# Batch index 1 of an attention and feed-forward kernel: where three groups of vector work stand

## The chip, the core and the metric

The kernel runs on one core of one Trainium2 chip. The time is that of one execution of the whole program on the device, in microseconds. Four engines work beside each other and wait for each other through semaphores: PE multiplies matrices, DVE (VectorE) and ACT (ScalarE) do elementwise work, and SP issues the transfers between memory and the core. POOL (GpSimd) does almost nothing here.

## The reference

For each of 8 batch indices and 8 heads, 576 positions are softly assigned to 32 memory slots by `phi`; keys and values are averaged into these slots, the queries attend to them, and the joined heads (512 wide) go through a feed-forward layer with a SiLU. All of it is in float32.

```python
a = phi - np.max(phi, axis=2, keepdims=True)          # over the 576 positions
a = np.exp(a)
a = a / (np.sum(a, axis=2, keepdims=True) + 1e-09)
k_m = np.einsum('bhsm,bhsd->bhmd', a, k)
v_m = np.einsum('bhsm,bhsd->bhmd', a, v)
scores = np.matmul(q, k_m.transpose(0, 1, 3, 2)) / np.sqrt(64)
attn = softmax(scores)                                 # over the 32 slots
x = np.matmul(attn, v_m)                               # heads joined: 4608 x 512
h = x @ w_in                                           # 512 x 2048
out = (h * (1.0 / (1.0 + np.exp(-h)))) @ w_out         # 2048 x 512
```

## The kernel before, in words

**Batch index after batch index.** While the feed-forward work of index b runs on PE, the attention work of index b + 1 is done beside it in small steps, its *events*. For index 1, which this text is about, the feed-forward work is cut into 16 *slots* (`fc`), one for each 128 of the 2048 hidden columns.

**One slot of index 1.** PE forms the *first product* h (12 L701 matmuls over 2 x 288 positions). ACT applies the SiLU: L728 for 512 positions into a buffer g, L730 for the other 64 into `gleft`. For accuracy each f32 operand is held as a *high* part, rounded to the matmul's type, and a *remainder*. DVE writes g's high part (L718, a cast) and g's remainder (L720). Then the slot's events run, and then PE forms the *second product* of the slot before (12 L746 matmuls with the high and low parts of `w_out`). So the order on PE is: first product of slot s, steps of attention, second product of slot s - 1, first product of slot s + 1. There is a single tile for h, so that the next first product waits until L728 and L730 have read it.

**P.** The value part of attention is multiplied into `w_in` beforehand. Its result P is made in four parts, the events `p_mm` (L649 on PE, then L677, P's high part, on ACT, and L679, P's remainder, on DVE). Parts 1, 2 and 3 of index 1 are made in slots 1, 5 and 9, and read from slots 4, 8 and 12 on.

**The keys of index 2.** Its `phi` is loaded near the end of index 0's slots (SP, line 88), when DVE's transposes (L464) have freed the tile's home. Event `phi_max` in slot 1 takes a running maximum (L258, L259, L261 twice), `phi_fold` in slot 2 folds it over the partitions (L286 to L304) and `phi_sub` in slot 2.5 subtracts it (L312 and L315, twice each). The Exp (L319) is an ACT instruction between slots 3 and 4; each change between Exp and SiLU needs a table load on ACT. Event `e_tr` in slot 9 turns the averaged keys and values by PE into the free columns of h and copies them out: L368 for the keys, L369 for the values.

**The forms.** Events `w_forms` make eight *forms* of `w_out`, sums of its quarters that the later indices use. Form j starts in slot 1.5 j + 2 (the third in slot 5.5): on DVE a sum L814 and four more, L818 to L821; then on ACT their high parts (L835) and on DVE their remainders (L836). Form 0 comes in slot 2, form 1 in 3.5, form 5 in 9.5.

**What sets the order.** PE's order, and from index 1 on ACT's, is the order of the program text. DVE's order is made by a scheduler out of data dependences and its own estimate of when inputs are ready; `behind(i, other)` forbids it to put i ahead of other. `last_split[-1]` is the latest remainder of g, `last_p[-1]` the latest remainder of P. In the loop over slots, the names of DVE instructions that an event adds go into `late` if the event is in a list, and `late` instructions are put behind the slot's remainder of g.

Of the kernel before, what the change touches and what calls it, by code (L numbers as in the profile page):

```python
# [19 lines left out]
P = 128  # L20
# [28 lines left out]
def attn_ffn_kernel(  # L49
# [9 lines left out]
    nc = tc.nc  # L59
# [27 lines left out]
    def load(dst, src, few=False, queue=None):  # L87
        i = (queue or nc.sync).dma_start(dst, src)
        if few:
            tc.add_manual_dep(  # L90
                i.ins,
                loads[-DEEP].ins.name,
                mybir.DependencyInfo(mybir.DependencyClass.Sync, mybir.DependencyReason.DATA),
                reason="few at a time",
            )
        loads.append(i)

    @contextmanager
    def in_order(*engines):
        traced = nc.cur_bb.bb.instructions  # L100
        n = len(traced)
        last = {}
        yield last
        for i in list(nc.cur_bb.bb.instructions)[n:]:
            if i.engine in engines:
                if i.engine in last:
                    tc.add_manual_dep(
                        i,
                        last[i.engine].name,
                        mybir.DependencyInfo(mybir.DependencyClass.NoSync, mybir.DependencyReason.DATA),  # L110
                        reason="in_order",
                    )
                last[i.engine] = i
# [6 lines left out]
    raws, cvas, last_silu, last_split, last_kvn, last_turn = {}, {}, [], [], [], []  # L120
# [89 lines left out]
    def banks(b):  # L210
        if b == 0:
            return [ps.tile([P, 512], F32, tag="acc", name=f"first{i}", bufs=NI) for i in range(2)]
        bg = bgtile()
        return [bg[:, 0], bg[:, 1]]

    def beside_h(w):

        return [live["h"][:, i, HALF : HALF + w] for i in range(2)]
# [144 lines left out]
    def e_tr(b):  # L363
        pt = beside_h(P) if b <= 2 else banks(b)
        t = sb.tile([P, 2, NR, M], F32, tag="kvT", name=f"kvT{b}", bufs=2)
        for kind in range(2):
            nc.tensor.transpose(pt[kind][:, :P], kvn[:, kind].rearrange("p g d -> p (g d)"), ident)
        nc.vector.tensor_copy(t[:, 0].rearrange("p r m -> p (r m)"), pt[0][:, :P])  # L368
        nc.scalar.copy(t[:, 1].rearrange("p r m -> p (r m)"), pt[1][:, :P])  # L369
        at[b]["kvT"] = t  # L370

# [251 lines left out]
    pj, wins, last_p = {}, {}, []  # L623
# [173 lines left out]
    def as_f32(x):  # L797
        return x.bitcast(F32)

    def keep(tag, n):  # L800
        t = sb.tile([P, n, DMODEL], F32R, tag=tag, name="kept", bufs=1)
        for i in range(n):
            kept.append(t[:, i])
            kept_at.append((t, i))

    def w_forms(j, step):


        if step == 0:
            while len(kept) < 3 * j + 3:  # L810
                keep(*homes_left.pop(0))
            f = at[0]["forms", j] = sb.tile([P, 2, DMODEL], F32, tag="cva", name="wf", bufs=1)
            c = slice(2 * j, 2 * j + 2)
            i = nc.vector.tensor_tensor(f, as_f32(wo_hi[:, c]), as_f32(wo_lo[:, c]), op=ALU.add)  # L814
            if j < 3:
                behind(i.ins, last_kvn[0] if j == 2 else last_split[-1])
            b11, b12, b21, b22 = (f[:, k, q * Q : (q + 1) * Q] for k in range(2) for q in range(2))
            nc.vector.tensor_tensor(b11, b12, b11, op=ALU.subtract)  # L818
            nc.vector.tensor_tensor(b12, b22, b12, op=ALU.add)
            nc.vector.tensor_tensor(b22, b22, b11, op=ALU.add)  # L820
            nc.vector.tensor_tensor(b21, b22, b21, op=ALU.subtract)  # L821
            return
        f = at[0]["forms", j].rearrange("p k (q f) -> p (k q) f", q=2)
        t1 = sb.tile([P, 1, DMODEL], F32R, tag="cva1", name="t1", bufs=1)
        runs = [[t1, 0, 1]]
        for u in range(3 * j, 3 * j + 3):
            t, i = kept_at[u]
            if t is runs[-1][0]:
                runs[-1][2] = i + 1
            else:  # L830
                runs.append([t, i, i + 1])
        n = 0
        for t, i, e in runs:
            src, to = f[:, n : n + e - i], t[:, i:e]
            nc.scalar.activation(to[:, :, :Q], src, AF.Copy)  # L835
            nc.vector.tensor_tensor(to[:, :, Q:], src, to[:, :, :Q], op=ALU.subtract)  # L836
            n += e - i
        load(saved[j], as_f32(t1[:, 0]))
# [6 lines left out]
    def ffn1s(b, t, j):  # L845
        h = live["h"] = ps.tile([P, 2, 512], F32, tag="h", name="h", bufs=1)
        ahi, alo = (at[b][x][:, :, t * HALF : (t + 1) * HALF] for x in ("ahi", "alo"))
        hi, lo = pj[b, j // 2]
        for i in range(2):
            f = (2 * j + i) * P % JW  # L850
            n = 0
            for wt, a in ((hi, ahi), (hi, alo), (lo, ahi)):
                for p in range(2):
                    nc.tensor.matmul(  # L854
                        h[:, i, :HALF], wt[:, p, f : f + P], a[:, p], start=n == 0, stop=n == 5
                    )
                    n += 1
        return h
# [393 lines left out]
    def behind(i, other):  # L1252
        tc.add_manual_dep(
            i,
            other.ins.name,
            mybir.DependencyInfo(mybir.DependencyClass.NoSync, mybir.DependencyReason.DATA),
            reason="behind",
        )

    def finish(tiles):  # L1260
        if prev is None:
            return
        if prev[0] == "main":
            main_step(prev[1], prev[2], prev[3], tiles)
        elif prev[0] == "left" and tiles[0] == 0:
            if prev[1] < 2:
                left_step(prev[1], prev[2], prev[3])
                t1_load(prev[2])
            else:
                left_st(prev[1], prev[2], prev[3])  # L1270
        elif prev[0] == "st" and tiles[0] == 0:
            st_step(*prev[1:])
# [16 lines left out]
    for b in range(B):  # L1289
        if b == 1:  # L1290
            whole.close()
            ctx.enter_context(in_order(ACT))
        for s in range(NFC if b > 1 else 0):
            t, j = divmod(s, NP)
            h = ffn1s(b, t, j)
            part = forms(b, t, j, h)
            run(b, s)
            finish(range(NI))
            prev = ("st", b, t, j, part)
        for fc in range(NFC if b < 2 else 0):  # L1300
            if b == 0 and fc < 2:
                for part in range(2):
                    for fn, a in events.pop((b, fc + part / 2), []):
                        fn(*a)
                continue
            h = ffn1(b, fc, low_last=b == 1 and fc == 0)
            gs = split(silu(b, fc, h), steps=(2, 1) if fc == NFC - 1 else (0, 1))
            for part in range(2):
                if b == 0:
                    finish((2 * part, 2 * part + 1))  # L1310
                traced = nc.cur_bb.bb.instructions
                n = len(traced)
                late = set()
                for fn, a in events.pop((b, fc + part / 2), []):
                    m = len(nc.cur_bb.bb.instructions)
                    fn(*a)
                    if fn is phi_max or b and fn in (s_max, s_sub, s_sum, s_norm, s_back, s_low):
                        late.update(i.name for i in list(nc.cur_bb.bb.instructions)[m:])
                if b == 0:
                    for i in list(nc.cur_bb.bb.instructions)[n:]:  # L1320
                        if i.engine == ACT:
                            behind(i, last_silu[-1])
                        elif i.engine == DVE and (fc > 10 or i.name in late):
                            behind(i, last_split[-1])
                for i in list(nc.cur_bb.bb.instructions)[n:] if b else ():
                    if i.engine == DVE and i.name in late:
                        behind(i, last_split[-1])
            if b:
                finish(range(NI))
            prev = ("main", b, fc, gs)  # L1330
        if b % 2:
            for n in range(NLS):
                gs = left_split(b, n)
                run(b, NFC + n)
                finish((0, 1, 2, 3))
                prev = ("left", b, n, gs)
# [56 lines left out]
```

## Time and profile before

| | us |
|---|---|
| median of 3 runs | 682.2 (681.66 to 682.36) |
| the profiled execution | 681.68 |
| its span in the trace | 679.9 |
| PE busy | 666.5 (98%) |
| DVE busy | 518.6 (76%) |
| ACT busy | 370.1 (54%) |
| first product of slot 0 of index 1 begins | 105.75 |
| first product of index 2 begins | 201.74 |

A profile row gives the start, the length, the engine, the source line, the operation, `out<-in` by tile names and the shape; `x12` means that twelve instructions are shown as one. What stands in brackets is the idle time of the engine just before, and what ended it. Rows of the waits give the waiting group, whom it waited for, the total, the number and the longest. Instructions of one engine overlap a little, so that the next can start before the length of the last is over.

### The profile page before, as it was taken

The numbers are of one execution on the slowest core, as the hardware profiler recorded it, in microseconds if no ns is written. First come the engines' busy times: TensorE is split into PE (matmuls) and PEld (weight loads), VectorE is DVE, ScalarE is ACT, GpSimd is POOL, SyncE is SP. The second block draws the span as 40 slices with busy tenths as digits, with TensorE's granted clock in tenths as the row PEclk, the third lists the DMA queues.
The fourth block names the chain that finished last, engine by engine and source line by source line (L and its number), as shares of the span: only waits on it lengthen the run. The fifth ranks groups of instructions, "written<-read, shape, count | busy, mean of one in ns | idle before, by whom it ended". The sixth has DMA issues, their size and how long they took to land.

```text
span 679.9 us, 14538 instructions
## 1 busy us (share of the span) xinstructions
PE 666.5 (98%) x5792; PEld 589.8 (87%) x5792; DVE 518.6 (76%) x1093; ACT 370.1 (54%) x685; POOL 0.7 (0%) x6
## 2 busy tenths in 40 slices
PE   7999999899999999999999999999999999999997
PEld 3687778687879998999988999899996999889996
DVE  4997897888958688868877678887977668867653
ACT  3878684433535646554654646564654546554541
POOL 0000000000000000000000000000000000000000
PEclk9999999899999999999999999999999999999999
DMA  9998975133271443243430524216431204210001
GB/s 340 368 339 275 322 294 204 50 110 99 89 252 47 183 157 124 79 143 126 173 132 16 184 73 169 101 35 243 156 125 34 86 2 156 95 45 17 32 1 47
DMA packets 37907, 93.92 MB, mean 138 GB/s; under 512 B 4688, under 2 KB 21456, under 8 KB 34256
## 3 DMA queue, kind: packets, MB, share of 16 engines
q1 hardware_dynamic: 36816, 90.22, 38.1%
q10 hardware_dynamic: 1024, 2.77, 1.0%
q8 instruction: 46, 0.75, 0.5%
q14 instruction: 21, 0.17, 0.1%
HBM read 77.22 MB, written 15.73 MB: 137 GB/s over the span
## 4 chain that ended last, share of the span: by engine, by line
PE 85%; DVE 4%; issue 1%; ACT 1%; DMA 0%; ACTq 0%; DVEq 0%
PE sum L893 36%; PE h L854 22%; PE acc L746 7%; PE h L701 5%; PE lsum L977 5%; PE bg L649 3%; PE accleft L746 2%; PE bg L335 1%; PE bg L382 1%; PE h L335 1%; PE pacc L649 1%; DVE wf L814 1%; DVE kept L836 0%; DMA out<-o 0%; DVE gparts L720 0%
## 5 line engine op out<-in xcount | busy, mean ns | idle before, releaser
L854 PE MATMUL h<-aparts,pm 128*128 128x288 f32 x1152 | 168.5, 295 | 0.0
L854 PEld LDWEIGHTS h<-aparts,pm 128*128 128x128 f32 x1152 | 157.4, 188 | 0.5
L868 ACT ACTIVATE gbuf<-h 128x512 f32<-128x512 f32 x96 | 57.3, 597 | 116.8 <-PE h L854 114.2
L893 PE MATMUL sum<-wo_hi,aparts 128*128 128x256 f32 x384 | 102.3, 289 | 0.0
L893 PE MATMUL sum<-kept,aparts 128*128 128x256 f32 x576 | 100.1, 282 | 0.0
L893 PE MATMUL sum<-wo_lo,aparts 128*128 128x256 f32 x384 | 100.0, 282 | 0.0
L873 DVE TENSOR_TENSOR gbuf<-gbuf 128x256 f32<-128x256 f32 x96 | 40.6, 423 | 69.0 <-ACT gbuf L868 68.6
L882 ACT ACTIVATE aparts<-gbuf 128x512 fp32r<-128x512 f32 x86 | 54.4, 633 | 62.1 <-DVE gbuf L877 62.1
L746 PE MATMUL acc<-wo_hi,gparts 128*128 128x512 f32 x256 | 85.1, 397 | 0.0
L893 PEld LDWEIGHTS sum<-kept,aparts 128*128 128x128 f32 x576 | 82.5, 191 | 0.0
L893 PEld LDWEIGHTS sum<-wo_hi,aparts 128*128 128x128 f32 x384 | 72.7, 189 | 9.8 <-ACT gleft L870 7.5
L884 DVE TENSOR_TENSOR gparts<-gbuf,aparts 128x512 fp32r<-128x512 f32 x86 | 59.6, 693 | 19.6 <-ACT aparts L882 19.6
L893 PE MATMUL sum<-wo_hi,gparts 128*128 128x256 f32 x384 | 73.2, 281 | 0.0
L893 PEld LDWEIGHTS sum<-wo_lo,aparts 128*128 128x128 f32 x384 | 73.1, 190 | 0.0
L893 PE MATMUL sum<-kept,gparts 128*128 128x256 f32 x288 | 65.5, 282 | 0.0
L701 PEld LDWEIGHTS h<-aparts,pm 128*128 128x128 f32 x372 | 52.3, 190 | 10.5 <-ACT gleft L730 4.0
L701 PE MATMUL h<-aparts,pm 128*128 128x288 f32 x372 | 56.8, 302 | 4.0 <-ACT gleft L730 2.9
L893 PEld LDWEIGHTS sum<-wo_hi,gparts 128*128 128x128 f32 x384 | 59.4, 190 | 0.0
L746 PEld LDWEIGHTS acc<-wo_hi,gparts 128*128 128x128 f32 x256 | 48.3, 190 | 11.6 <-issue 1.0
L872 ACT ACTIVATE aparts<-gbuf 128x384 fp32r<-128x384 f32 x96 | 50.4, 525 | 0.0
L746 PE MATMUL acc<-wo_lo,gparts 128*128 128x512 f32 x128 | 49.6, 395 | 0.4 <-DVE wo_lo L182 0.4
L893 PEld LDWEIGHTS sum<-kept,gparts 128*128 128x128 f32 x288 | 47.9, 190 | 0.0
(225 smaller groups left out, 956.9 us busy)
## 6 DMA issues: line engine op xcount, KB each, us to landing
win<-win_saved SPq DMA_DIRECT2D x24, 1024.0 KB, 5.0
kv<-in_kv SPq DMA_DIRECT2D x28, 516.0 KB, 5.0
q<-in_q SPq DMA_DIRECT2D x16, 576.0 KB, 6.3
raw<-in_w_in SPq DMA_DIRECT2D x14, 512.0 KB, 7.6
raw<-in_w_out SPq DMA_DIRECT2D x6, 1024.0 KB, 6.5
win_saved<-win SPq DMA_DIRECT2D x4, 1024.0 KB, 8.6
phi<-in_phi SPq DMA_DIRECT2D x7, 576.0 KB, 8.5
out<-oo SPq DMA_DIRECT2D x26, 128.0 KB, 1.9
```

What stands on the lines that cost most here:

```text
L335: nc.tensor.matmul(pt[p][M * r : M * (r + 1), :KVW], e[:, p, c, M * r : M * (r + 1)], kvt[c][:, p, r], start=c == 0, stop=False, skip_grou ...
L649: nc.tensor.matmul((bg[p][M * r : M * (r + 1)] if beside else bg[M * r : M * (r + 1), p, :w]).rearrange("p (k f) -> p k f", f=P), kvT[D * ...
L701: nc.tensor.matmul(h[:, hf, :HALF], wt[:, p, fs], a[:, p, hf * HALF : (hf + 1) * HALF], start=n[hf] == 0, stop=n[hf] == 5, skip_group_chec ...
L746: nc.tensor.matmul(acc[key], gt[:, cs], wt[:, fc], start=fc == 0 and n == 0, stop=fc == NFC - 1 and n == 2)
L854: nc.tensor.matmul(h[:, i, :HALF], wt[:, p, f : f + P], a[:, p], start=n == 0, stop=n == 5)
L868: nc.scalar.activation(gbuf[:, :MAIN].rearrange("p (i f) -> p i f", i=2), h[:, :, :w], AF.Silu)
L872: nc.scalar.activation(hi[:, :3], g[:, 1:4], AF.Copy)
L873: nc.vector.tensor_tensor(g[:, 4:6], g[:, :1].broadcast_to([P, 2, P]), g[:, 1:3], op=ALU.subtract)
L882: nc.scalar.activation(hi[:, 3:], g[:, 4:], AF.Copy)
L884: last_split.append(nc.vector.tensor_tensor(lo[:, 3:], g[:, 4:], hi[:, 3:], op=ALU.subtract))
L893: nc.tensor.matmul(sums[bank][:, place * Q : (place + 1) * Q], gt[:, k], wt, start=bank not in begun, stop=True, skip_group_check=True,)
L977: nc.tensor.matmul(sums[k], part[gt][:, 2 * i + k], wt[:, fc], start=n == 0 and i == 0 and m == 0, stop=True, skip_group_check=True,)
```

## The change

Three edits, all for work beside index 1. The maximum over `phi` of index 2 is no longer put behind g's remainder of slot 1 (index 1's maximum, beside index 0, still is). The copy of index 2's turned keys goes from DVE to ACT. The first sum of form 5 (j == 5, slot 9) is put behind the latest remainder of P.

```diff
@@ e_tr, line 368
-        nc.vector.tensor_copy(t[:, 0].rearrange("p r m -> p (r m)"), pt[0][:, :P])
+        (nc.scalar.copy if b == 2 else nc.vector.tensor_copy)(t[:, 0].rearrange("p r m -> p (r m)"), pt[0][:, :P])
@@ w_forms, line 815
-            if j < 3:
-                behind(i.ins, last_kvn[0] if j == 2 else last_split[-1])
+            if j < 3 or j == 5:
+                behind(i.ins, last_kvn[0] if j == 2 else last_p[-1] if j == 5 else last_split[-1])
@@ the loop over slots, line 1317
-                    if fn is phi_max or b and fn in (s_max, s_sub, s_sum, s_norm, s_back, s_low):
+                    if fn is phi_max and not b or b and fn in (s_max, s_sub, s_sum, s_norm, s_back, s_low):
```

What this does to the order is not in the diff, since the scheduler lays out DVE. On DVE, from the last remainder of index 0 (the first row) on, there stood before: cast and remainder of slots 0 and 1, then the maximum (`phi2`, `mt`, `mx`), P's remainder (`pm`) and the fold.

```order
L720 TENSOR_TENSOR gparts_79<-gbuf_82,gparts_79 128x512
L718 CAST gparts_79<-gbuf_82 128x512
L720 TENSOR_TENSOR gparts_79<-gbuf_82,gparts_79 128x512
L718 CAST gparts_79<-gbuf_82 128x512
L720 TENSOR_TENSOR gparts_79<-gbuf_82,gparts_79 128x512
L258 TENSOR_TENSOR mt_1233<-phi2_1109 128x512
L259 TENSOR_TENSOR mx_1232<-mt_1233 128x256
L261 TENSOR_TENSOR mx_1232<-mx_1232,phi2_1109 64x128
L679 TENSOR_TENSOR pm_1229<-bg_1220,pm_1229 128x1024
L261 TENSOR_TENSOR mx_1232<-mx_1232,phi2_1109 64x128
L286 STREAM_TRANSPOSE mxt_1278<-mx_1232 128x256
L288 TENSOR_REDUCE qm_1280<-mxt_1278 128x8
```

Now, on DVE from the same remainder on:

```order
L720 TENSOR_TENSOR gparts_79<-gbuf_82,gparts_79 128x512
L258 TENSOR_TENSOR mt_1233<-phi2_1109 128x512
L259 TENSOR_TENSOR mx_1232<-mt_1233 128x256
L261 TENSOR_TENSOR mx_1232<-mx_1232,phi2_1109 64x128
L718 CAST gparts_79<-gbuf_82 128x512
L261 TENSOR_TENSOR mx_1232<-mx_1232,phi2_1109 64x128
L720 TENSOR_TENSOR gparts_79<-gbuf_82,gparts_79 128x512
L286 STREAM_TRANSPOSE mxt_1278<-mx_1232 128x256
L288 TENSOR_REDUCE qm_1280<-mxt_1278 128x8
L294 COPY qz_1282<-qm_1280 32x8 x4
L296 TENSOR_REDUCE fm_1287<-qz_1282 32x8
L298 COPY fm_1287<-fm_1287 32x8 x3
```

The maximum stands ahead of slot 0's cast, and the fold between slot 0's remainder and slot 1's cast. Further on, on DVE at slot 2, there stood before (L304 ends the fold; cast and remainder are those of slot 2, `wf` is form 0):

```order
L304 STREAM_TRANSPOSE am_1292<-wide_1293 128x256
L718 CAST gparts_79<-gbuf_82 128x512
L312 TENSOR_TENSOR phi2_1109<-phi2_1109,am_1292 128x512
L720 TENSOR_TENSOR gparts_79<-gbuf_82,gparts_79 128x512
L814 TENSOR_TENSOR wf_1272<-wo_hi_76,wo_lo_77 128x1024
L315 TENSOR_TENSOR phi2_1109<-phi2_1109,am_1292 64x128
L818 TENSOR_TENSOR wf_1272<-wf_1272 128x256
L312 TENSOR_TENSOR phi2_1109<-phi2_1109,am_1292 128x512
L819 TENSOR_TENSOR wf_1272<-wf_1272 128x256
L836 TENSOR_TENSOR t1_1296<-wf_1272,t1_1296 128x256
L820 TENSOR_TENSOR wf_1272<-wf_1272 128x256
L315 TENSOR_TENSOR phi2_1109<-phi2_1109,am_1292 64x128
```

And now on DVE, from slot 1's cast (first row) through slot 2's (sixth row) into form 0:

```order
L718 CAST gparts_79<-gbuf_82 128x512
L312 TENSOR_TENSOR phi2_1109<-phi2_1109,am_1292 128x512
L720 TENSOR_TENSOR gparts_79<-gbuf_82,gparts_79 128x512
L315 TENSOR_TENSOR phi2_1109<-phi2_1109,am_1292 64x128
L679 TENSOR_TENSOR pm_1229<-bg_1220,pm_1229 128x1024
L718 CAST gparts_79<-gbuf_82 128x512
L720 TENSOR_TENSOR gparts_79<-gbuf_82,gparts_79 128x512
L814 TENSOR_TENSOR wf_1272<-wo_hi_76,wo_lo_77 128x1024
L818 TENSOR_TENSOR wf_1272<-wf_1272 128x256
L819 TENSOR_TENSOR wf_1272<-wf_1272 128x256
L836 TENSOR_TENSOR t1_1296<-wf_1272,t1_1296 128x256
L820 TENSOR_TENSOR wf_1272<-wf_1272 128x256
```

The subtractions stand beside slot 1's cast and remainder, P's remainder behind them, and form 0's sums follow each other. At slot 9 there stood before on DVE, from its cast on (`wf` is form 5):

```order
L718 CAST gparts_79<-gbuf_82 128x512
L814 TENSOR_TENSOR wf_1658<-wo_hi_76,wo_lo_77 128x1024
L720 TENSOR_TENSOR gparts_79<-gbuf_82,gparts_79 128x512
L679 TENSOR_TENSOR pm_1649<-bg_1640,pm_1649 128x1024
L368 COPY kvT2_1652<-h_1623 128x128
L818 TENSOR_TENSOR wf_1658<-wf_1658 128x256
```

And now:

```order
L718 CAST gparts_79<-gbuf_82 128x512
L720 TENSOR_TENSOR gparts_79<-gbuf_82,gparts_79 128x512
L679 TENSOR_TENSOR pm_1649<-bg_1640,pm_1649 128x1024
L814 TENSOR_TENSOR wf_1658<-wo_hi_76,wo_lo_77 128x1024
L818 TENSOR_TENSOR wf_1658<-wf_1658 128x256
```

The form's first sum went behind both remainders, and the copy left DVE. On ACT it stands between P's high part and the copy of the values. PE's and SP's instructions keep their order.

## The prediction

> **What bounds the kernel now.** I read first which engine is full to the end, then who made PE wait in index 1, then the longest wait engine by engine, and last the granted clock there. The busy time of each engine from 165 to 679 us:
>
> ```profile
> 165.00:679.00 514.00, 510.91 (x4542) 472.23 (x4540) 384.68 (x849) 268.66 (x519) 0.00 (x0) 1.00 0.31 106
> ```
>
> PE (the first pair) is busy in 510.91 of these 514.00 us, so what index 1 saves ahead of 165 us should pass through to the end, and a shorter DVE or ACT is worth only what PE waits for it. From 105 to 200 us PE's two longest waits are:
>
> ```profile
> PE h L701 <- ACT gleft L730: 2.9, 1, 2.9
> PE h L701 <- ACT kvT L369: 0.7, 1, 0.7
> ```
>
> The first stands ahead of slot 4. PE's first products of slots 2, 3, 4 and 5 (each has the second product of the slot before behind it) start at:
>
> ```profile
> 115.74 1.75 PE L701 MATMUL h<-aparts,pm 128*128 128x288 f32 x12
> ...
> 120.07 1.75 PE L701 MATMUL h<-aparts,pm 128*128 128x288 f32 x12
> ...
> 127.42 2.60 PE L701 MATMUL h<-aparts,pm 128*128 128x288 f32 x12 [2.86 <-ACT gleft L730]
> ...
> 133.40 1.75 PE L701 MATMUL h<-aparts,pm 128*128 128x288 f32 x12
> ```
>
> An undisturbed slot takes 120.07 - 115.74 = 4.33 us. The next two take 7.35 and 5.98, so 3.02 + 1.65 = 4.67 us are lost. The 1.65 is the clock (third figure from the end), which fell after the wait:
>
> ```profile
> 130.00:131.00 1.00, 1.00 (x4) 0.81 (x3) 0.90 (x4) 0.89 (x1) 0.00 (x0) 0.50 0.00 0
> ```
>
> Who made slot 4 wait? ACT, which works in the order of the program:
>
> ```profile
> 125.93 0.84 ACT L835 ACTIVATE kept<-wf 128x768 fp32r<-128x768 f32 x1 [2.02 <-DVE wf L821]
> 126.68 0.58 ACT L728 ACTIVATE gbuf<-h 128x512 f32<-128x512 f32 x1
> 127.16 0.21 ACT L730 ACTIVATE gleft<-h 128x64 f32<-128x64 f32 x1
> 127.39 1.28 ACT L319 ACT_TABLE_LOAD   x1
> 128.68 1.16 ACT L319 ACTIVATE phi<-phi 128x1152 f32<-128x1152 f32 x1
> 130.11 1.28 ACT L728 ACT_TABLE_LOAD   x1 [0.26 <-PE h L701]
> ```
>
> Slot 3's two silu instructions (L728, L730) stood behind the high parts of form 0, and those waited 2.02 us for DVE's last form sum. The products h have one tile, so slot 4 can start when L730 has read it. DVE was late because index 2's key weights stood among its form sums:
>
> ```profile
> 117.07 0.45 DVE L286 STREAM_TRANSPOSE mxt<-mx 128x256 f32<-128x256 f32 x1
> ...
> 120.21 0.39 DVE L718 CAST gparts<-gbuf 128x512 fp32r<-128x512 f32 x1
> 120.51 0.68 DVE L312 TENSOR_TENSOR phi<-phi,am 128x512 f32<-128x512 f32 x1
> 121.11 0.69 DVE L720 TENSOR_TENSOR gparts<-gbuf,gparts 128x512 fp32r<-128x512 f32 x1
> 121.71 1.22 DVE L814 TENSOR_TENSOR wf<-wo_hi,wo_lo 128x1024 f32<-128x1024 f32 x1
> 122.85 0.28 DVE L315 TENSOR_TENSOR phi<-phi,am 64x128 f32<-64x128 f32 x1
> 123.05 0.41 DVE L818 TENSOR_TENSOR wf<-wf 128x256 f32<-128x256 f32 x1
> ...
> 124.32 0.41 DVE L836 TENSOR_TENSOR t<-wf,t 128x256 fp32r<-128x256 f32 x1
> ...
> 125.42 0.43 DVE L821 TENSOR_TENSOR wf<-wf 128x256 f32<-128x256 f32 x1
> ...
> 128.81 1.22 DVE L814 TENSOR_TENSOR wf<-wo_hi,wo_lo 128x1024 f32<-128x1024 f32 x1
> ...
> 131.45 0.43 DVE L821 TENSOR_TENSOR wf<-wf 128x256 f32<-128x256 f32 x1
> ```
>
> From 117.07 to 120.21 DVE folds the maximum (3.14 us) while slot 2's cast L718 waits. Then the subtractions L312 and L315 stand between L814 and L821: 3.71 us apart in form 0, 2.64 in form 1, where none stand between.
>
> **Part 1: the maximum no longer ordered behind slot 1's remainder.** It needs phi of index 2, and DVE.
>
> ```profile
> 104.55 0.33 SPq L88 DMA_DIRECT2D phi<-in_phi  x1
> ```
> ```profile
> DMA to landing us min/median/max: 3.8/3.8/3.8
> ```
> ```profile
> 106.88 0.69 DVE L720 TENSOR_TENSOR gparts<-gbuf,gparts 128x512 fp32r<-128x512 f32 x1
> ...
> 113.00 0.43 DVE L718 CAST gparts<-gbuf 128x512 fp32r<-128x512 f32 x1 [3.13 <-ACT gbuf L728]
> 113.53 0.69 DVE L720 TENSOR_TENSOR gparts<-gbuf,gparts 128x512 fp32r<-128x512 f32 x1
> 114.14 0.68 DVE L258 TENSOR_TENSOR mt<-phi 128x512 f32<-128x512 f32 x1
> ...
> 115.53 1.21 DVE L679 TENSOR_TENSOR pm<-bg,pm 128x1024 fp32r<-128x1024 f32 x1
> ```
>
> Phi lands at 104.55 + 3.8 = 108.35; DVE is free at 107.57. So L258 starts near 108.4 instead of 114.14, ahead of the 3.13 us in which DVE stood idle. This adds a wait: behind L258 stands slot 0's cast, and behind the cast PE's second product of slot 0. The maximum up to the cast takes 115.53 - 114.14 = 1.39 us, so the cast comes at 109.8. PE reaches that product only behind slot 1's first, whose silu of 0.6 us ended ahead of 113.00, so not before 112.3: 2 us cover it.
>
> From cast to remainder DVE needs 0.53, from remainder to the next 0.61 (the rows of 113.00 to 114.14), so the fold starts at 110.9 and ends at 114.1. Then, from start to start, come two L312 (0.60), two L315 (0.20), slot 1's cast (0.30) and remainder (0.60) among them, and L679 from 116.6 to 117.8. PE needs slot 1's remainder at about 117.4, behind slot 2's first product; it ends near 116.7. Slot 2's product ends at 117.49, its silu 0.6 later, so its cast starts at 118.15, not at 120.21. L814 follows 0.53 + 0.60 behind, at **119.3, 2.4 us earlier**.
>
> Without subtractions L821 follows L814 after form 1's 2.64 and the row of t, 0.41 at most: 3.0 instead of 3.71. So L821, the high parts and slot 3's silu come 3.1 us earlier, and L730 ends at 127.37 - 3.1 = 124.25. PE wants slot 4 at 120.07 + 4.33 = 124.40: **no wait, by 0.15 us, and no low clock**.
>
> What is late next is the Exp. Its table load starts at 124.25 and the Exp ends 128.68 + 1.16 - 127.39 = 2.45 later, at 126.7; the second table load (1.28) and slot 4's silu pair (127.16 + 0.21 - 126.68 = 0.69) end at 128.7. PE wants slot 5 at 124.40 + 4.33 = 128.73: level. I count slot 5 at 128.75 against 133.40, **4.65 us**. Bounds: 4.67 (the whole loss) and 3.0 (the clock's 1.65 stays, should small gaps remain).
>
> The Trainium skill (TensorE: Matmul & The Clock Gate, Part 1: The HAM clock gate) lets the clock fall after an idle window of about 3.4 us; by that, 2.86 us would not have cost the 1.65, and the sum would be that much smaller. The trace shows 0.50 after 2.86, so the measurement decides.
>
> **Parts 2 and 3, slot 9.** All engines in order of time, and one end of a product without a wait behind it:
>
> ```profile
> 124.17 0.39 PE L746 MATMUL acc<-wo_hi,gparts 128*128 128x512 f32 x1
> ```
> ```profile
> 157.21 1.03 ACT L677 ACTIVATE pm<-bg 128x1024 fp32r<-128x1024 f32 x1
> ...
> 157.39 0.42 DVE L718 CAST gparts<-gbuf 128x512 fp32r<-128x512 f32 x1
> ...
> 160.17 0.39 PE L746 MATMUL acc<-wo_hi,gparts 128*128 128x512 f32 x1
> 160.60 0.28 DVE L368 COPY kvT<-h 128x128 f32<-128x128 f32 x1
> ...
> 160.92 0.27 ACT L369 COPY kvT<-h 128x128 f32<-128x128 f32 x1 [2.68 <-DVE kvT L368]
> 161.23 1.86 PE L701 MATMUL h<-aparts,pm 128*128 128x288 f32 x12 [0.67 <-ACT kvT L369]
> ```
>
> The turned keys lie in h, so slot 10 waits for both copies, and DVE's copy stood behind a form's sum and two remainders. On ACT it follows L677, at 158.25; by the row of L369 each copy takes 0.27, so both end by 158.9, ahead of PE's 160.17. Slot 4 was wanted at 124.40, 0.23 behind the start at 124.17; so slot 10 starts at 160.40 instead of 161.23: **0.83 us**. ACT pays its 0.27 out of 2.68 idle. The form behind P's remainder: remainder 157.9, L679 158.5, L814 159.7, its first sum 1.25 later at 160.95, where in before the copy held it until 160.88. Its four sums end by 162.8, and slot 10's cast cannot come before 160.40 + 1.75 + 0.6 = 162.75, so nothing waits longer. Bounds: 0.6 (something of the wait left) and 0.95 (the product's 1.86 back at 1.75).
>
> **Sum.** 4.65 + 0.83 = 5.48 us. The profiled execution took 681.68 us (span 679.9), which gives 676.2; the median of the runs, 682.2, lies 0.5 above, which gives 676.7. I take **676.5**. The transfers of index 1 are issued on these engines' progress and move with them.
>
> **Rivals.**
> **(a) The wait comes back behind the Exp.** Between slots 3 and 4 ACT has nothing to spare, so any excess there is a wait of PE in slot 5. For it speaks the exact balance; against it that the Exp starts 1.29 us behind the start of a table load of 1.28, with nothing hidden between. Should each of the two loads cost once more its 1.28 when no wait covers it, the gain falls by 2.6: 679.1. The Trainium skill (ScalarE: Activation LUTs, What ACT_TABLE_LOAD costs) counts load and drain, about 2.66 us a switch, which is this rival; the trace agrees with its load and shows no drain.
> **(b) Slower: DVE stands at L258 for phi.** Slot 4 follows L814 by 5 us (119.3 to 124.25), so in before's place it would need L814 by 122.45; L814 follows L258 by 10.65 once slack is gone. A landing after 111.8 thus loses slot 4's gain, and one after 112.6 slot 9's too. The page's row of all phi loads speaks for it:
>
> ```profile
> phi<-in_phi SPq DMA_DIRECT2D x7, 576.0 KB, 8.5
> ```
>
> With 8.5 us phi lands at 113.05, slot 4 comes 1.2 us later than before, and with slot 9's 0.83 the time is 682.1 to 682.6. PE also waits 2 us for slot 0's cast; if that lowers the clock as the 2.86 did, 1.65 more: 684. Against it: this very load took 3.8, and nothing ahead of it changes.
> **(c) DVE's sums were not what held ACT.** If the high parts wait for something as late, a transfer out of their home, only slot 9 counts: 680.9. Against it: L821 ends at 125.85 and ACT starts at 125.93.
>
> **How the numbers follow.** The forecast gets 0.82; the bounds of its terms, 5.6 and 3.6, give 676.1 to 678.1 by the profiled execution, and with the 0.7 by which the runs differ below it 675.4 to 678.2. The rivals get (a) 0.07, (b) 0.06, (c) 0.05. The range is the forecast's own; (a) to (c) stay out with 0.18. About 0.2% (1.4 us) can be told from no change: faster 0.89 (forecast and a), same 0.07 (c, a third of b), slower 0.04 (the rest of b).
>
> **What would show it.** Right: L258 near 108.4, slot 0's cast near 109.8, form 0's L814 near 119.3; slot 4's first product 4.3 to 4.5 us behind slot 3's, at a clock of 1; L368 on ACT right behind L677, and no wait for kvT ahead of slot 10; from there all about 5.5 us earlier. Wrong: DVE waiting for phi beyond 111, PE waiting for gleft ahead of slot 5, a clock below 1 after 124 us, or waits of PE after 165 us that were not there.

## The result, and the profile after

| | before | changed |
|---|---|---|
| median of 6 runs, us | 682.12 (680.09 to 682.72) | 676.77 (676.18 to 677.24) |
| profiled execution, us | 681.68 | 677.24 |
| its span, us | 679.9 | 675.5 |
| first product of slot 0 of index 1 begins | 105.75 | 106.28 |
| first product of index 2 begins | 201.74 | 197.31 |
| the stretch between these two | 95.99 | 91.03 |

The ratio is 0.9924, with a 95% interval of 0.9911 to 0.9938: 5.35 us faster by the medians. Executions reach slot 0 of index 1 up to 0.7 us apart, whatever the kernel: 105.61 to 106.33 in all traces of this study, and 105.72 to 106.33 in the three of the kernel before alone. The stretch from slot 0 to index 2 leaves that out; it became 4.96 us shorter, and from here on it is the measure for traces.

Who made PE wait in the changed kernel, from 100 to 200 us:

```profile
PE h L367 <- ACT gleft L730: 0.4, 1, 0.4
PE h L701 <- ACT gleft L730: 0.2, 1, 0.2
```

The waits of 2.9 and 0.7 us are gone; 0.2 us of the first is left. The wait of 0.4 us at L367 stood in the kernel before too, with the same length. The first products of slots 2 to 5 on PE:

```profile
116.27 1.75 PE L701 MATMUL h<-aparts,pm 128*128 128x288 f32 x12
...
120.61 1.75 PE L701 MATMUL h<-aparts,pm 128*128 128x288 f32 x12
...
125.27 1.86 PE L701 MATMUL h<-aparts,pm 128*128 128x288 f32 x12 [0.17 <-ACT gleft L730]
...
129.77 1.86 PE L701 MATMUL h<-aparts,pm 128*128 128x288 f32 x12
```

From first product to first product, slots 3 and 4 now take 4.66 and 4.50 us, where they took 7.35 and 5.98: 4.17 of the 4.67 us above two undisturbed slots came back. DVE shows why, from index 0's last remainder on:

```profile
107.40 0.68 DVE L720 TENSOR_TENSOR gparts<-gbuf,gparts 128x512 fp32r<-128x512 f32 x1
109.25 0.69 DVE L258 TENSOR_TENSOR mt<-phi 128x512 f32<-128x512 f32 x1 [1.16 <-DMA phi<-in_phi]
...
110.64 0.41 DVE L718 CAST gparts<-gbuf 128x512 fp32r<-128x512 f32 x1
...
118.03 1.22 DVE L679 TENSOR_TENSOR pm<-bg,pm 128x1024 fp32r<-128x1024 f32 x1
119.17 0.42 DVE L718 CAST gparts<-gbuf 128x512 fp32r<-128x512 f32 x1
119.69 0.69 DVE L720 TENSOR_TENSOR gparts<-gbuf,gparts 128x512 fp32r<-128x512 f32 x1
120.30 1.22 DVE L814 TENSOR_TENSOR wf<-wo_hi,wo_lo 128x1024 f32<-128x1024 f32 x1
...
123.26 0.43 DVE L821 TENSOR_TENSOR wf<-wf 128x256 f32<-128x256 f32 x1
```

The maximum runs as soon as phi has landed, after a wait of 1.16 us, and slot 0's cast follows it. That wait is not all spare time: ACT ended slot 0's silu at 108.77, so the cast stood ready for its last 0.5 us. PE did not have to wait for it, since it reaches slot 0's second product only at 113.40. L814 to L821 of form 0 take 2.96 us instead of 3.71. ACT is then in time:

```profile
123.77 0.85 ACT L835 ACTIVATE kept<-wf 128x768 fp32r<-128x768 f32 x1 [1.34 <-DVE wf L821]
124.52 0.58 ACT L728 ACTIVATE gbuf<-h 128x512 f32<-128x512 f32 x1
125.00 0.22 ACT L730 ACTIVATE gleft<-h 128x64 f32<-128x64 f32 x1
125.23 1.28 ACT L319 ACT_TABLE_LOAD   x1
126.53 1.17 ACT L319 ACTIVATE phi<-phi 128x1152 f32<-128x1152 f32 x1
127.71 1.28 ACT L728 ACT_TABLE_LOAD   x1
129.01 0.60 ACT L728 ACTIVATE gbuf<-h 128x512 f32<-128x512 f32 x1
129.50 0.22 ACT L730 ACTIVATE gleft<-h 128x64 f32<-128x64 f32 x1
```

The second table load no longer waits for PE, as it did at 130.11. Now ACT's round trip (table load, Exp, table load, silu pair) ends at 129.72 and sets slot 5 at 129.77, 4.50 us behind slot 4. At slot 9 all engines, in order of time:

```profile
153.70 1.03 ACT L677 ACTIVATE pm<-bg 128x1024 fp32r<-128x1024 f32 x1
...
154.60 0.28 ACT L368 COPY kvT<-h 128x128 f32<-128x128 f32 x1
...
154.75 0.30 ACT L369 COPY kvT<-h 128x128 f32<-128x128 f32 x1
...
155.01 1.22 DVE L679 TENSOR_TENSOR pm<-bg,pm 128x1024 fp32r<-128x1024 f32 x1
...
156.15 1.21 DVE L814 TENSOR_TENSOR wf<-wo_hi,wo_lo 128x1024 f32<-128x1024 f32 x1
...
156.66 0.39 PE L746 MATMUL acc<-wo_hi,gparts 128*128 128x512 f32 x1
...
156.89 1.75 PE L701 MATMUL h<-aparts,pm 128*128 128x288 f32 x12
```

Both copies are done at 155.05, 1.8 us ahead of slot 10, which starts 0.23 us behind the start of the last L746. Slots 9 and 10 take 6.17 + 5.74 us, where they took 6.99 + 5.85: 0.93 us.

### The profile page after: what moved, and what is told of

It reads as the page before. It is cut to its first block, busy times and chain, and to the rows that moved or that the text cites. A ratio compares the mean times of both kernels' runs of the same rounds, so it can differ in the third digit from the quotient of the medians.

```text
span 675.5 us, 14539 instructions
## 1 busy us (share of the span) xinstructions
PE 665.1 (98%) x5792; PEld 588.5 (87%) x5792; DVE 518.6 (77%) x1092; ACT 370.2 (55%) x686; POOL 0.7 (0%) x6
## 4 chain that ended last, share of the span: by engine, by line
PE 79%; DVE 6%; issue 1%; ACT 1%; DMA 1%; DVEq 0%; ACTq 0%
PE sum L893 36%; PE h L854 23%; PE lsum L977 5%; PE acc L746 4%; PE bg L649 3%; PE h L701 2%; PE accleft L746 2%; PE bg L382 1%; PE h L335 1%; PE bg L335 1%; PE pacc L649 1%; DMA phi<-in_phi 1%; DVE gparts L720 1%; DVE wf L814 1%; DVE gparts L718 0%
## 5 line engine op out<-in xcount | busy, mean ns | idle before, releaser
L746 PE MATMUL acc<-wo_hi,gparts 128*128 128x512 f32 x256 | 84.4, 394 | 0.0
L746 PEld LDWEIGHTS acc<-wo_hi,gparts 128*128 128x128 f32 x256 | 47.8, 188 | 11.5 <-issue 1.0
L746 PE MATMUL acc<-wo_lo,gparts 128*128 128x512 f32 x128 | 49.3, 393 | 0.4 <-DVE wo_lo L182 0.4
```

The source lines that it names most:

```text
L746: nc.tensor.matmul(acc[key], gt[:, cs], wt[:, fc], start=fc == 0 and n == 0, stop=fc == NFC - 1 and n == 2)
```

## The experiments

**Each edit alone.** First the maximum (line 1317) alone:

```diff
-                    if fn is phi_max or b and fn in (s_max, ...
+                    if fn is phi_max and not b or b and fn in (s_max, ...
```

> The kernel before with the first edit alone (the maximum over phi of index 2 not put behind slot 1's remainder). My theory: form 0's sums come earlier, slots 4 and 5 start 4.3 to 4.7 us behind the slot before, no low clock, and 4.2 to 4.7 us are gained: near 677.7 where the kernel before takes 682.1. Slot 9 keeps its wait of 0.7 us for the turned keys. Rival (the lateness of DVE's sums was not what held ACT): within 0.5 us of the kernel before, slot 4 still more than 7 us behind slot 3.

Measured: 677.23 us, ratio 0.9937 (0.9923 to 0.995), beside 681.68 for the kernel before on the same chip. On PE slot 4 came 4.33 and slot 5 another 4.51 us behind the slot before:

```profile
119.92 1.75 PE L701 MATMUL h<-aparts,pm 128*128 128x288 f32 x12
...
124.25 1.87 PE L701 MATMUL h<-aparts,pm 128*128 128x288 f32 x12
...
128.76 1.86 PE L701 MATMUL h<-aparts,pm 128*128 128x288 f32 x12
```

The 0.7 us wait for kvT stayed. So the first edit alone brings about 4.5 us (4.4 of the stretch, which took 91.58), and DVE's lateness was what held ACT; the rival (c) of the prediction falls. Then the copy (line 368) alone and the form (line 815) alone:

```diff
+        (nc.scalar.copy if b == 2 else nc.vector.tensor_copy)(t[:, 0] ...
```

> The kernel before with the second edit alone (the copy of the turned keys on ACT). My theory: slot 10 no longer waits for kvT, 0.8 us gained, near 681.3, with the 2.9 us wait ahead of slot 4 untouched. Rival (ACT or DVE late elsewhere takes it back by slot 12): nothing gained, slots 10 to 12 together as long as before.

```diff
+            if j < 3 or j == 5:
+                behind(i.ins, last_kvn[0] if j == 2 else last_p[-1] if j == 5 else last_split[-1])
```

> The kernel before with the third edit alone (form 5's first sum behind P's remainder; the copy stays on DVE and, by the scheduler's order, then stands right behind g's remainder of slot 9). My theory: the copies end near 159 on the clock of the kernel before, ahead of the 160.4 at which PE wants slot 10, so that this edit alone gives the same 0.8 us as the copy on ACT. Rival (the copy must leave DVE): a wait of 0.3 us or more for kvT stays.

Measured: 680.27 us (ratio 0.9979, 0.9969 to 0.999) and 681.16 us (0.999, 0.998 to 1.0), beside the same 681.68. Both were expected near 0.8 us; the medians give 1.4 and 0.5, and they can't be taken as they stand, for a reason that the next experiments show (the clock). In the traces slots 9 and 10 together take 11.89 us with the copy alone and 11.90 with the form alone, against 12.84 before. With the form alone DVE and ACT copy in time too:

```profile
157.90 0.69 DVE L720 TENSOR_TENSOR gparts<-gbuf,gparts 128x512 fp32r<-128x512 f32 x1
...
158.51 0.28 DVE L368 COPY kvT<-h 128x128 f32<-128x128 f32 x1
...
158.83 0.27 ACT L369 COPY kvT<-h 128x128 f32<-128x128 f32 x1 [0.61 <-DVE kvT L368]
...
160.39 1.75 PE L701 MATMUL h<-aparts,pm 128*128 128x288 f32 x12
```

Either edit does the whole work at this place. The changed kernel with the copy back on DVE says the same of the form's edit:

```diff
-        (nc.scalar.copy if b == 2 else nc.vector.tensor_copy)(t[:, 0] ...
+        nc.vector.tensor_copy(t[:, 0] ...
```

> The changed kernel with the copy of the turned keys back on DVE. By my theory the second and third edits do the same work twice: no wait for kvT ahead of slot 10, and within 0.3 us of the changed kernel's 676.8. Rival (the copy on ACT is what counts): 0.5 to 0.8 us slower than the changed kernel.

Measured: 676.82 us (0.993, 0.9917 to 0.9942), stretch 90.93 us, no wait for kvT. The copy on ACT adds nothing to the form's new place. (The first two edits together, without the third, were not run.)

**Is the second loss the clock?** Twelve matmuls on a constant fill the wait ahead of slot 4 in the kernel before:

```diff
+            if b == 1 and fc == 4:
+                keep_warm(bgtile().rearrange("p b f -> p (b f)")[:, :512], 12)
             h = ffn1(b, fc, low_last=b == 1 and fc == 0)
```

> The kernel before with 12 extra matmuls on a constant, ahead of slot 4's first product, into a PSUM tile that nothing reads; they fill the 2.86 us in which PE waits there. The wait itself stays. My theory (the loss of 4.67 us is 3.0 of waiting and 1.65 of a lower clock afterwards): slot 5 comes 4.3 to 4.5 us behind slot 4 instead of 5.98, the granted clock stays at 1, and 1.2 to 1.65 us are gained: near 680.6. Rival (the 1.65 is not the clock but the Exp and table loads on ACT): slot 5 still 5.5 us or more behind slot 4 and nothing gained.

Measured: 680.76 us against 681.89 on the same chip (0.9984, 0.9974 to 0.9995), so 1.1 us, and on PE:

```profile
124.32 2.76 PE L80 MATMUL bg<-ident 128*128 128x512 bf16 x12
127.23 1.86 PE L701 MATMUL h<-aparts,pm 128*128 128x288 f32 x12 [0.15 <-ACT gleft L730]
```

Slot 5 came 4.51 us behind slot 4 and not 5.98, with the same table loads on ACT. Each run's record also holds its mean granted clock: 0.999 or 1.0 in all ten runs with the matmuls, but 0.994 to 0.997 in 11 of the 13 runs of the kernel before beside them. So the loss was the clock, and the matmuls prevent it. But the trace of the copy alone had shown a second thing: the 2.9 us wait was there, and slot 5 came 4.50 us behind slot 4 all the same. So the kernel before was profiled in two more executions.

> The kernel before once more, one look at its clock. The wait of 2.86 us ahead of slot 4 must be there again. If the clock falls after every such wait, slot 5 follows slot 4 by 5.7 to 6.0 us; if it falls in some executions only, by 4.5 us in some of them, with the span 1.2 to 1.6 us shorter.

> A third look at the kernel before, with the same two readings: slot 5 at 5.7 to 6.0 us behind slot 4 where the clock fell, at 4.5 where it did not.

Measured: 680.76 and 680.2 us, with waits of 2.7 and 2.8 us ahead of slot 4, slot 5 at 4.51 and 4.50 us, and stretches of 94.49 and 94.56 us. The granted clock (third figure from the end) from 128 to 129 us in the form alone, in the copy alone and in the kernel before's second execution, in that order:

```profile
128.00:129.00 1.00, 1.00 (x6) 1.00 (x6) 0.90 (x2) 0.99 (x2) 0.00 (x0) 0.50 0.00 0
```
```profile
128.00:129.00 1.00, 1.00 (x9) 1.00 (x9) 0.91 (x2) 0.99 (x2) 0.00 (x0) 1.00 0.00 0
```
```profile
128.00:129.00 1.00, 1.00 (x8) 1.00 (x9) 0.90 (x3) 1.00 (x1) 0.00 (x0) 1.00 0.00 0
```

Of five traces with an idle PE of 2.7 to 3.0 us ahead of slot 4, the clock fell in two (the kernel before's first and the form alone) and held in three. A fall costs 95.99 - 94.5 = 1.5 us by the traces of the kernel before, and 94.93 - 93.75 = 1.2 us by those of the form alone (it fell) and the copy alone (it held), which at slots 9 and 10 are alike.

How often does an execution pay? The recorded clocks tell. Of the 40 runs of the kernel before beside these experiments, on three chips, 31 show 0.994 to 0.997 (median 681.95 us) and 9 show 1.0 (median 680.52): about three in four pay, some 1.4 us each. The six sets of runs of kernels with the first edit and phi on time, 30 runs, show 0.999 or 1.0 throughout, so the fall belongs to the wait ahead of slot 4. The recorded clocks also sort the runs behind the two medians above. With the copy alone the clock fell in four runs of eight, with the form alone in eight of eleven, for the kernel before on that chip in 14 of 18. Where it held, the copy alone is 1.3 us faster than the kernel before and the form alone 1.1; where it fell, 1.2 and 0.7. These lie around the 0.9 us of the traces, with three to fourteen runs in each group.

**When does phi's landing decide?** Stores of an unused copy ahead of phi's load delay it. The maximum is held by hand ahead of slot 0's cast, where it stands in the changed kernel, so that the scheduler does not let the cast pass when phi comes later.

```diff
+    def hold_back(b):
+        for k in range(1):          # 2 in the second kernel
+            load(hbm.tile([P, 2, S], F32, name=f"spare{k}"), at[b]["aT"][ALL])
...
+            if len(first_max) == 1:
+                behind(i.ins, first_max[0])
```

> The changed kernel with the maximum held by hand ahead of slot 0's cast, and one more store (0.56 MB of the transposed scores to a spare place that nothing reads) ahead of phi's load in SP's queue, so that phi lands some 2 us later. By the rival that the landing decides (DVE stands at the maximum), slot 4 follows the maximum by 16 us: each us of later landing costs one, so 2 us of the gain go, 678.5 to 679.5, and PE has no wait ahead of slot 0's second product yet. If the landing has slack: within 0.5 us of the changed kernel.

> The same with two such stores ahead of phi's load, so that it lands some 4 us later than in the changed kernel. By the rival that the landing decides: PE waits 1 to 2 us for slot 0's cast, slot 4 starts 23 us behind slot 0 (18.99 in the changed kernel, 21.67 before), and with the clock falling after it the time is 680.8 to 683, about that of the kernel before or slower. If the landing has slack: under 678.

Measured: 678.01 us (0.9942, 0.9925 to 0.9958) and 679.26 us (0.9956, 0.9941 to 0.9971). The stores shifted the landing less than I had estimated, so the first lies below the 678.5 to 679.5 expected: the maximum started 4.01 and 5.96 us behind slot 0's first product, where in the two traces of the changed kernel it was 2.97 and 2.67. In the second, DVE waited for phi and PE then twice (added lines shift the numbers: L263 is the maximum, L708 the first and L756 the second product, L725 the cast):

```profile
DVE mt L263 <- DMA phi<-in_phi: 4.2, 1, 4.2
```
```profile
PE h L708 <- ACT gleft L740: 1.3, 1, 1.3
PE acc L756 <- DVE gparts L725: 1.2, 1, 1.2
```

Slot 4 followed the maximum by 16.0 us in the changed kernel, 15.97 in the first and 15.68 in the second. Against the second trace of the changed kernel (90.73), a landing 1.34 and 3.29 us later cost 1.29 and 2.92 us of the stretch: 0.9 to 1 us for each. So the landing has no slack, and the mechanism of rival (b) is real. Its size was off in my expectation of 680.8 to 683 for the second: slot 4 came 21.64 us behind slot 0 and not 23, because phi was 3 us later and not 4, and the clock held. Carried on by this slope, which no run does, the kernel before with its clock held (94.5) is reached at a landing some 4 us later than in the changed kernel, which is where the prediction put it (112.6 against 108.35).

**A kernel less tied to the landing.** P's remainder of part 1 is read only in slot 4. Put behind form 0's last sum, it no longer stands ahead of slot 2's cast:

```diff
+            ev(b, 1, p_high, b, JW)
...
+                    ev(b, 2, p_low, b, JW)
...
+        behind(last_p[0].ins, last_form[0])
```

> The changed kernel with P's remainder of part 1 put behind form 0's last sum instead of ahead of slot 2's cast. In the changed kernel's trace slots 4 and 5 still take 4.66 and 4.50 us, 0.5 over the undisturbed 4.33, because slot 2's cast starts 0.5 us later than its silu allows. My theory: both slots return to 4.33 to 4.4, and 0.3 to 0.5 us are gained, 676.3 to 676.5. Rival (P's remainder then delays form 0's remainders and slot 3's cast): slot 3's second product waits, and nothing is gained.

> P's remainder of part 1 behind form 0's last sum, beside the changed kernel on one chip. My theory: slots 4 and 5 at 4.33 to 4.40 us each whatever phi's landing within a microsecond, 0.3 to 0.6 us faster than the changed kernel. Rival: its four runs near 676.1 were the chip or chance, and both kernels agree within 0.2 us.

> The changed kernel once more, for a comparison on one chip with the kernel that has P's remainder behind form 0. 676.5 to 677.2 by its six runs so far; slots 4 and 5 together 8.8 to 9.2 us, depending on when phi lands (108.2 to 109.3 in the traces so far).

Measured: 676.11 us (0.9909, 0.9894 to 0.9924), and then beside the changed kernel on one chip 676.65 (0.9924, 0.9911 to 0.9938) against 676.82 (0.993, 0.9917 to 0.9942). The two cannot be told apart by time: of the 0.3 to 0.6 us expected, the medians on one chip show 0.17. In the traces slots 3 and 4 take 4.33 and 4.36 us both times, although the maximum started 2.89 and 2.85 us behind slot 0, and the stretch is 90.58 us both times. The changed kernel's was 91.03 with phi late (4.66 and 4.50) and 90.73 with phi early (4.36 and 4.50). The kernel with the copy back on DVE, whose maximum started 2.89 us behind slot 0 too, took 4.57 and 4.51. On DVE slot 2's cast (L725 here) now waits for its silu, not for P:

```profile
118.05 0.43 DVE L725 CAST gparts<-gbuf 128x512 fp32r<-128x512 f32 x1 [0.77 <-ACT gbuf L735]
```

So it is 0.15 to 0.45 us better by the traces and has the shortest stretch of the study; the times don't show it, and phi was not made later with it.

## Why the prediction held

- **The chain behind slot 4** was named right: slot 4 waited for the silu pair, that for the forms' high parts, those for DVE. Taking index 2's key weights out of the forms' way removed it, alone (max_only) and with the rest.
- **The maximum in idle time.** Forecast: L258 at 108.4, slot 0's cast at 109.8, L814 at 119.3. In the trace, less the 0.53 us by which slot 0 came later: 108.72, 110.11, 119.77. Phi landed 4.2 us after its issue at 105.07, not 3.8, which made the maximum 0.32 us late. DVE's chain from the maximum to P's remainder (L679) was also mis-sized: 8.78 us (109.25 to 118.03), where I had 8.2 (108.4 to 116.6). Of these 0.58 us, 0.23 is the second L261, which runs between slot 0's cast and remainder and which the sum left out. I had P's remainder done 0.35 us ahead of slot 2's cast; in the trace the cast waits for it, and so L814 came 0.47 late. That ate the 0.15 us I had left to slot 4 and 0.3 more: slot 3 took 4.66 us, and 4.36 in the second trace of the kernel, where phi was early.
- **The Exp as what is late next.** I called it level with PE (4.35 us for slot 5's step). It is the bound: 4.50 us in the changed kernel, and about 4.45 is what my own rows of ACT give from one L730 to the next. The error was to let it start ahead of slot 4, while slot 4 starts at that same L730. It is 0.15 us, and the kernel before pays it too: where its clock held, slot 4 took 4.51 and 4.50 us. Nothing hidden stands between the table loads: rival (a) did not come.
- **The clock.** I took 1.65 us as part of every execution, by one trace. The loss was real in that trace, but 1.48 us of it are the clock (5.98 against 4.50) and the rest is ACT's round trip, and it comes in some executions only: two of the five traces with 2.7 to 3.0 us of idle PE, and 31 of 40 runs of the kernel before. That the trace I read was one of these was luck. The forecast came out since the median execution of before pays the fall; against an execution that does not, the gain is 94.5 - 91 = 3.5 us. By the Trainium skill (TensorE: Matmul & The Clock Gate, Part 1: The HAM clock gate) the clock falls after an idle window of about 3.4 us, and that window is free-running. I set this aside by one trace. The three traces that held agree with the Trainium skill. The two that fell do not, as it stands: PE had been idle for 2.86 us in all in the one, and for 2.5 us in the other when the clock fell (124.66 to 127.2). Whether the place of the gap in such a window decides, these runs don't show.
- **Slot 9.** Forecast 0.83, bounds to 0.95; measured 0.93. The product's return from 1.86 to 1.75 us, by which slot 10 became 0.11 shorter, is the difference. That the copy alone would do was right; that the form's new place alone does it too I had not said.
- **The sum.** 5.48 us were forecast; the traces give 4.17 + 0.93 us for the two places, of which 0.1 is lost again in slot 5 (7.95 us after 7.84; the kernel before also has 7.95 where its clock held). That is the 4.96 us of the stretch; with the second trace of the changed kernel it is 5.26, and the medians give 5.35. That forecast and medians agree to 0.13 us is partly luck, since the first term was 0.48 too large by the first trace. Nothing was given back later: from index 2's first product to the end of the span both kernels take 478.2 us.

## What to carry to other kernels

Work without a due time belongs where the engine stands idle, but a profile must tell for what it now waits: here each microsecond by which phi lands later costs about one, and by that slope the gain would be used up some 4 us later. Of two edits that free the same wait, try each alone; here the copy on ACT is needless. And where PE's clock falls after a wait in some executions only, one profile shows one of two outcomes: take several, and read the recorded clock of every run, before a clock term enters a sum.

## What the runs showed of the hardware

An idle PE of 2.7 to 3.0 us lowered the granted clock to 0.50 in two traces of five and left it at 1.00 in three. The low clock lasted 3.4 us in both: from 128.2 to 131.6 in the kernel before, where it began 0.8 us after PE was busy again, and from 127.2 to 130.6 with the form alone, where it began 0.4 us before. It is seen in the recorded clock of 31 of 40 runs of the kernel before. With idle times of 1.2 and 1.3 us ahead of slot 4 the two traces with phi late kept 1.00; but one of the four runs of the first, of which there is no trace, shows 0.997 and took 678.91 us, 0.9 more than the others' median. Twelve matmuls (128x512, bf16) in the gap kept the clock at 1.00 in the trace and at 0.999 or 1.0 in all ten runs. A table load on ACT was followed by its activation 1.29 to 1.30 us after its start in the traces shown.
